# A transformer block on one core: the first four queries computed before the shift, all weight sums on VectorE, modulation weights loaded one group ahead

## The chip, the cores and the metric

The kernel runs on one core of one Trainium2 chip. The metric is the device time of one execution in microseconds (us). All runs named here are fast ones (granted clock 0.995 to 1.0 on the core). A profile is of one execution, so single stretches of it can differ from the median run by a few us.

In the profile PE is TensorE's matmuls, PEld its weight loads, DVE VectorE, ACT ScalarE, POOL GpSimd, SPq the instruction queue of SyncE, which issues nearly all DMAs here. L257 would be line 257 of the program. Line numbers differ between the kernels, because the change adds lines: VectorE's modulation sum is L699 before and L748 after, and the subtraction of weight blocks is L500 before and L541 after.

## The reference

```python
mod = (silu(c) @ w_mod)                     # six rows of 1024: sa, ca, ga, sb, cb, gb
h = layernorm(x) * (1 + ca) + sa            # x: 2048 x 1024, bfloat16
x = x + ga * attention(h)                   # 32 query heads, 4 key heads of 128, last 512 keys
h = layernorm(x) * (1 + cb) + sb
x = x + gb * ((silu(h @ w_gate) * (h @ w_up)) @ w_down)     # 3584 wide
```

The attention projects queries with `wq` (1024 x 4096) and its output with `wo`.

## The kernel before

Tokens are handled in four chunks of 512. In a chunk, 32 heads pass one after another. TensorE works for head `i` (scores, probabilities times values) and for the queries of heads `i+4` and later. From head 8 the queries of two heads come from seven smaller products instead of eight (a Strassen-like scheme), which needs differences of blocks of `wq`, the *weight sums*. They are computed in the first chunk, four per group of four heads, stored to DRAM, and loaded again in later chunks. In the first chunk VectorE also has to move products out of PSUM, normalise the next chunk, and sum up the modulation weights.

```python
def weight_sums(g, st, e, which):            # st, e: the engine; each is 128x1024
    ...
    for k in which:
        x, y, extra = ((b12, b11, []), (b22, t_[:, 0], [bt[0]]), (b22, b12, []), (b21, t_[:, 1], [bt[1]]))[k]
        tt_(st, e, t_[:, k], bt[k], x, y, ALU.subtract, B_wq[sl] + extra)
# in the loop over heads, at the end of head i:
if i % 4 == 3 and i > 3:  load_wq((i + 1) // 4 + 2)         # 1 MB of query weights, two DMAs
g = (i + 6) // 4
if i % 4 == 2 and 2 <= g < HG + 2:
    if g > 2: weight_sums(g, DVE, V, (0,))
    weight_sums(g, POOL, G, (2,))            # GpSimd
g = (i + 5) // 4
if i % 4 == 3 and 2 <= g < HG + 2:
    if g > 2: weight_sums(g, DVE, V, (1,))
    weight_sums(g, POOL, G, (3,))            # GpSimd
if i % 4 == 0 and i >= 4 and (i + 4) // 4 < HG + 2:
    store_sums((i + 4) // 4)                 # 1 MB to DRAM
# at the start of a head in the first chunk:
if h < 12: load_x(TPC + h)                   # 256 KB
if h in (8, 10, 12): load_wo((h - 8) // 2)   # 1 MB of output weights
```

At the start, 2048 columns of `w_mod` (shift and scale, 4 MB) are loaded, and the first query waits for both halves:

```python
for kc in (0, 1, 2, 3, 6, 7):  ln_scale(0, kc, g1, B_g1, sa, B_sa)      # h = n * g1 + sa
...
qproj(0); qproj(1, XBK); turn_keys(); qproj(2); scores(0); qproj(3, XBK)
```

Every instruction is recorded with the semaphores it has to wait for. In the traces below VectorE goes through its list in order: an instruction that could run stands behind one that waits, in one place behind a wait of 4.06 us.

The softmax here doesn't subtract the row's maximum and nothing guards it: scores larger than these inputs give would overflow.

## Time and profile before

| | us |
|---|---|
| median of the four runs beside the changed kernel | 1276.68 (1273.82 to 1279.53) |
| profiled span | 1274.5 |
| first query product | 20.15 |
| first exponential of head 5 to that of head 31 | 104.0 |
| the same 13 pairs of heads at the later chunks' 6.60 us a pair | 85.8 |

The page of the kernel before gives busy time by engine, and then busy tenths in 40 slices of the span:

```profile
PE 1240.5 (97%) x8129; PEld 710.8 (56%) x8269; DVE 622.8 (49%) x1265; ACT 370.4 (29%) x500; POOL 53.9 (4%) x57
...
PE   6988999999999999999999999999999999999999
...
DVE  4888704987048871377504643145422553133421
...
POOL 1322300000000000000000000000000000000000
PEclk9999999999999999999999999999999999999999
```

TensorE is below 9 tenths only within the first four slices (127 us). VectorE is at 4 to 8 tenths there, and GpSimd shows in the first five alone. VectorE's 49% over the whole span says nothing about that stretch.

The timeline of ScalarE of the kernel before (start, duration, what), with the exponentials of heads 5 and 31, and of two heads a pair apart in the second chunk:

```profile
46.33 1.94 ACT L608 ACTIVATE arena<-ps 128x1024 bf16<-128x1024 f32 x2
...
150.29 1.94 ACT L608 ACTIVATE arena<-ps 128x1024 bf16<-128x1024 f32 x2
...
232.45 1.94 ACT L608 ACTIVATE arena<-ps 128x1024 bf16<-128x1024 f32 x2
...
239.06 1.94 ACT L608 ACTIVATE arena<-ps 128x1024 bf16<-128x1024 f32 x2
```

The exponential follows TensorE's scores, so it serves as a clock of the heads: 8.0 us for a pair in the first chunk, 6.6 later.

What TensorE waited for between 20 and 200 us (who, for whom, us in total, times, longest):

```profile
PE ps L259 <- DVE arena L557: 9.2, 6, 2.8
PE ps L259 <- DVE arena L624: 1.6, 3, 0.9
...
```

L557 is a copy of a product out of PSUM. That copy takes 0.42 us, so longer waits mean that VectorE came to it late. Three timelines of one stretch show why: GpSimd's, then VectorE's, then TensorE's, with the wait of 1.58 us in its bracket:

```profile
61.10 2.12 POOL L500 TENSOR_TENSOR arena<-arena 128x1024 f16<-128x1024 bf16 x1 [1.19 <-DVE arena L500]
```

```profile
61.27 2.50 DVE L699 SCALAR_TENSOR_TENSOR arena<-arena 128x512 f32<-128x512 bf16 x1
...
64.15 0.41 DVE L557 COPY arena<-ps 128x256 f32<-128x256 f32 x1
```

```profile
64.62 10.49 PE L259 MATMUL ps<-arena 128*128 128x256 f16 x103 [1.58 <-DVE arena L557]
```

While GpSimd forms its weight sum, VectorE's modulation step, with both inputs in SBUF, takes 2.50 us instead of 0.74. It ends 0.55 us after the sum, so it seems to have stood until GpSimd was done. Beside another sum (at 71.4 us) a subtraction with both inputs in SBUF takes 1.86 us instead of 0.68 and also ends 0.55 us after it, while a multiplication with an operand from PSUM keeps its 0.69. Four of the six waits follow such a stretched instruction; the longest, 2.8 us, has another cause. A second sort of wait, in VectorE's timeline, where the bracket is the idle time before an instruction and what ended it:

```profile
96.42 0.49 DVE L695 TENSOR_SCALAR arena<-arena 128x512 f32<-128x512 bf16 x1 [3.52 <-DMA arena<-in_w_mod_dram]
96.86 0.42 DVE L557 COPY arena<-ps 128x256 f32<-128x256 f32 x1
```

VectorE stands 3.52 us for a load of modulation weights that nobody needs soon. Behind it in the queue stands the copy that TensorE does need: this is the wait of 2.8 us, and from 96.85 us the granted clock is half for 3.41 us.

### The profile page before, as it was taken

The page shows a single profiled execution, that of the slowest core. Times are in us where ns is not written, and L with a number is a line of the kernel's source. Part 1 is how long each engine was busy: PE and PEld are TensorE (multiplying, and loading weights), DVE is VectorE, ACT ScalarE, POOL GpSimd, SP SyncE. Part 2 cuts the span into 40 slices and gives each one's busy share as a digit, 9 for nine tenths or more (in the row PEclk, how much of TensorE's full clock was granted, in tenths as well). Part 3 has the DMA queues.
Part 4 walks back from the last instruction along what each step waited for, and adds up shares of the span by engine and source line. Part 5 has one row for each costly group of instructions (what it writes and reads, how often), then busy time and mean ns, then how long its engine had stood idle before and what let it go on. Part 6 is the DMA issues. An engine that isn't in the chain of part 4 may idle for free.

```text
span 1274.5 us, 20165 instructions
## 1 busy us (share of the span) xinstructions
PE 1240.5 (97%) x8129; PEld 710.8 (56%) x8269; DVE 622.8 (49%) x1265; ACT 370.4 (29%) x500; POOL 53.9 (4%) x57
## 2 busy tenths in 40 slices
PE   6988999999999999999999999999999999999999
PEld 3666645777457774578744444444444444444444
DVE  4888704987048871377504643145422553133421
ACT  2655502676026770177700111011100111011100
POOL 1322300000000000000000000000000000000000
PEclk9999999999999999999999999999999999999999
DMA  7997545997549995488448974036520645024200
GB/s 265 252 313 210 180 136 178 292 255 206 167 159 262 250 216 145 147 238 214 89 147 285 299 215 155 25 83 161 178 92 25 157 148 179 28 83 133 67 9 25
DMA packets 234846, 212.50 MB, mean 167 GB/s; under 512 B 106752, under 2 KB 205952, under 8 KB 230912
## 3 DMA queue, kind: packets, MB, share of 16 engines
q1 hardware_dynamic: 234736, 211.19, 58.3%
q8 instruction: 65, 1.06, 0.4%
q14 instruction: 29, 0.24, 0.1%
q10 hardware_dynamic: 16, 0.00, 0.0%
HBM read 174.07 MB, written 12.58 MB: 146 GB/s over the span
## 4 chain that ended last, share of the span: by engine, by line
PE 94%; DMA 2%; DVE 2%; issue 1%; SPq 0%; ACT 0%; DVEq 0%
PE ps L259 94%; DMA arena<-in_w_mod_dram 2%; DMA arena<-arena 0%; DVE arena L625 0%; SPq L276 0%; DVE arena L342 0%; DVE arena L500 0%; DVE arena L561 0%; DVE arena L557 0%; ACT arena L718 0%; SPq L269 0%; DVE arena L624 0%; DVE arena L594 0%; DVE arena L699 0%; DVE arena L363 0%
## 5 line engine op out<-in xcount | busy, mean ns | idle before, releaser
L259 PE MATMUL ps<-arena 128*128 128x512 bf16 (+4 forms) x8080 | 1236.7, 312 | 27.8 <-DVE arena L557 9.2
L259 PEld LDWEIGHTS ps<-arena 128*128 128x128 bf16 (+1 forms) x8220 | 707.0, 98 | 557.1 <-issue 13.5
L608 ACT ACTIVATE arena<-ps 128x1024 bf16<-128x1024 f32 x256 | 248.1, 1021 | 50.6 <-PE ps L259 47.7
L905 ACT ACTIVATE arena<-ps 128x512 bf16<-128x512 f32 x112 | 66.9, 597 | 518.0 <-PE ps L259 518.0
L635 DVE TENSOR_TENSOR arena<-ps,arena 128x512 bf16<-128x512 f32 (+1 forms) x65 | 44.4, 683 | 338.9 <-PE ps L259 338.9
L906 DVE SCALAR_TENSOR_TENSOR arena<-arena,ps 128x512 bf16<-128x512 bf16 x112 | 77.1, 688 | 142.1 <-ACT arena L905 142.1
L555 ACT ACTIVATE arena<-ps 128x256 f32<-128x256 f32 x120 | 46.0, 383 | 268.1 <-PE ps L259 268.1
L908 DVE SCALAR_TENSOR_TENSOR arena<-arena,ps 128x512 bf16<-128x512 bf16 x112 | 77.0, 687 | 53.7 <-PE ps L259 53.6
L625 DVE TENSOR_TENSOR arena<-ps,arena 128x512 bf16<-128x512 f32 x128 | 88.5, 691 | 4.7 <-DVE arena L624 0.2
L561 DVE TENSOR_TENSOR arena<-ps,arena 128x256 bf16<-128x256 f32 x180 | 75.4, 419 | 6.9 <-PE ps L259 2.2
L349 POOL TENSOR_TENSOR arena<-arena 128x1 f32<-128x1 f32 x32 | 18.2, 570 | 881.1 <-DVE arena L347 881.1
L699 DVE SCALAR_TENSOR_TENSOR arena<-arena 128x512 f32<-128x512 bf16 x56 | 47.2, 843 | 0.0
L624 DVE RECIPROCAL arena<-ps 128x4 f32<-128x4 f32 x128 | 23.1, 180 | 42.8 <-PE ps L259 42.0
L342 DVE BATCH_NORM_STATS2 arena<-arena 128x6 f32<-128x512 bf16 x64 | 43.9, 685 | 0.1
L500 POOL TENSOR_TENSOR arena<-arena 128x1024 f16<-128x1024 bf16 x16 | 34.4, 2149 | 86.4 <-DVE arena L500 45.3
L557 DVE COPY arena<-ps 128x256 f32<-128x256 f32 x60 | 25.2, 419 | 15.5 <-PE ps L259 15.4
L594 DVE CAST arena<-ps 128x256 bf16<-128x256 f32 x60 | 25.2, 420 | 13.3 <-PE ps L259 12.3
L637 DVE TENSOR_TENSOR arena<-arena 128x512 bf16<-128x512 bf16 (+1 forms) x65 | 27.4, 421 | 2.2
L500 DVE TENSOR_TENSOR arena<-arena 128x1024 f16<-128x1024 bf16 (+1 forms) x32 | 25.6, 809 | 0.2
L363 DVE TENSOR_SCALAR arena<-arena 128x512 bf16<-128x512 bf16 x62 | 22.4, 406 | 0.0
L353 DVE TENSOR_SCALAR arena<-arena 128x1024 bf16<-128x1024 bf16 x32 | 17.3, 540 | 2.9 <-DMA arena<-arena 2.4
L495 DVE CAST arena<-ps 128x512 bf16<-128x512 f32 x8 | 5.5, 687 | 7.6 <-PE ps L259 7.6
(31 smaller groups left out, 50.9 us busy)
## 6 DMA issues: line engine op xcount, KB each, us to landing
arena<-in_A_wq_dram SPq DMA_DIRECT2D x64, 512.0 KB, 4.8
arena<-in_A_wo_dram SPq DMA_DIRECT2D x32, 1024.0 KB, 5.3
arena<-in_B_w_gate_dram SPq DMA_DIRECT2D x28, 1024.0 KB, 5.3
arena<-in_B_w_up_dram SPq DMA_DIRECT2D x28, 1024.0 KB, 7.5
arena<-wq_sums SPq DMA_DIRECT2D x22, 1024.0 KB, 7.1
arena<-in_w_mod_dram SPq DMA_DIRECT2D x8, 1024.0 KB, 8.0
wq_sums<-arena SPq DMA_DIRECT2D x8, 1024.0 KB, 6.7
arena<-in_B_w_down_dram SPq DMA_DIRECT2D x4, 1792.0 KB, 11.0
```

What stands on the lines that cost most here:

```text
L259: T.op(PE, lambda: TE.matmul(out_ap, lhsT, rhs, start=start, stop=stop, skip_group_check=loose), reads=reads, writes=bb)
L342: T.op(DVE, lambda: V.bn_stats(st_sb[i][:, 6 * hf:6 * hf + 6], x_sb[:, t, 512 * hf:512 * hf + 512]), reads=[BX[t]], writes=[B_st[i]])
L500: T.op(st, lambda: e.tensor_tensor(dst, x, y, op), reads=reads, writes=[dst_b])
L555: T.op(ACT, lambda: A.activation(sn[k], bank(QBK, 256), AF.Copy), writes=PB[QBK] + [B_sn[k]])
L561: T.op(DVE, lambda: V.tensor_tensor(dst, bank(XBK, 256, off), sn[k], ALU.add), reads=[B_sn[k]], writes=PB[XBK] + [B_q[i % NQ]])
L608: T.op(ACT, lambda: A.activation(ex[i % NEX][:, kt:kt + 2, :], bank(SCB[kt], 1024).rearrange("p (a b) -> p a b", a=2), AF.Exp, scale=att_s ...
L625: T.op(DVE, lambda: V.tensor_tensor(o_sb[i % NOS].rearrange("p (a b) -> p a b", a=TPC), num, rl_bc, ALU.mult), reads=[B_rl], writes=both + ...
L635: T.op(DVE, lambda: V.tensor_tensor(tmp[s][:, 0:n], ps_ap, gate[:, lo:lo + n], ALU.mult), reads=[gate_b], writes=bb + [B_tmp[s]])
L699: T.op(DVE, lambda: V.scalar_tensor_tensor(acc, ms[:, kc, :], sc[:, kc:kc + 1], acc, op0=ALU.mult, op1=ALU.add), reads=[B_ms, B_sc, B_acc] ...
L905: T.op(ACT, lambda: A.activation(th[e], bank(gb_), AF.Tanh, scale=0.5), writes=PB[gb_] + [B_th[e]])
L906: T.op(DVE, lambda: V.scalar_tensor_tensor(out=t1[e], in0=th[e], scalar=1.0, in1=bank(gb_), op0=ALU.add, op1=ALU.mult), reads=[B_th[e]], w ...
L908: T.op(DVE, lambda: V.scalar_tensor_tensor(out=gu[:, ft, :], in0=t1[e], scalar=0.5, in1=bank(ub_), op0=ALU.mult, op1=ALU.mult), reads=[B_t ...
```

## The change

It starts the first four queries on the normalised and scaled but unshifted input, and adds the shift later as one column per head (`wq` transposed times `sa`), so only half of the first modulation load has to be waited for. It moves all weight sums to VectorE, one per head: the first two of each group a head earlier than before, the other two a head later. It loads modulation weights one group ahead and spreads their summing. It moves 14 PSUM copies to ScalarE. The core of the diff:

```diff
-            for kc in range(DT):
-                T.op(Q_wm[kc], lambda: SP.dma_start(wm[:, kc, :], w_mod[kc * P:(kc + 1) * P, 0:2 * D]), writes=[B_wm[kc]])
+            load_wm(0)                       # the scale half; then wq, keys
+            load_wm(1)                       # the shift half
...
-            qproj(0)
-            qproj(1, XBK)
-            turn_keys()
-            qproj(2)
-            scores(0)
-            qproj(3, XBK)
+            q_plain(0, Q0[0], 1)             # on the scaled input, no shift
+            q_plain(1, Q0[1], 1)
+            ... column products of the shift half, q_plain(2), turn_keys() ...
+            for i in range(4):
+                for kc in range(DT):
+                    mm(bank(SFT, 1, DT + i), wq_sb[0][:, kc, hd(i) * P:(hd(i) + 1) * P], sa[:, kc:kc + 1], ...)
+            T.op(DVE, lambda: V.tensor_copy(shift, bank(SFT, 4, DT)), writes=PB[SFT] + [B_shift])
+            for i in range(4):
+                if i == 3:
+                    q_plain(3, Q0[3], 1)
+                T.op(ACT, lambda: A.activation(q_sb[i], bank(Q0[i]), AF.Identity, bias=shift[:, i:i + 1]), ...)
...
-                snap(DVE, 1)
+                snap(ACT if p0 < Hq + LEAD else DVE, 1)
...
-                if h not in (Hq - 5, Hq - 4) and i > 2:
+                if ch == 0:
+                    for g_ in ([ln1[1]] if 1 in ln1 else []) + [mod_ga] * (i > 2) * (1 if i < 8 else i % 2 if i < 20 else 1 + i % 2):
+                        step(g_)
+                elif h not in (Hq - 5, Hq - 4):
                     run()
...
-                if i % 4 == 2 and 2 <= g < HG + 2:
-                    if g > 2:
-                        weight_sums(g, DVE, V, (0,))
-                    weight_sums(g, POOL, G, (2,))
-                (the same with sums 1 and 3 at i % 4 == 3)
-                if i % 4 == 0 and i >= 4 and (i + 4) // 4 < HG + 2:
-                    store_sums((i + 4) // 4)
+                for k in range(4):
+                    g = (i + 7 - k) // 4
+                    if i % 4 == (k + 1) % 4 and (3 if k < 2 else 2) <= g < HG + 2:
+                        weight_sums(g, DVE, V, (k,))
+                if i % 4 == 2 and i >= 6 and (i + 2) // 4 < HG + 2:
+                    store_sums((i + 2) // 4)
```

Cut: layer norm sums of two tiles on ScalarE, buffers and queues for the modulation loads, separate temporaries in `add_to_x`, the two exponentials of a head issued apart. The query-weight loads keep their places.

More of the change, by code (lines that the diff above doesn't have):

```diff
@@ L173, in bufs @@
         return [_Buf("%s%d" % (name, i)) for i in range(n)]
-    AT_WO, AT_OT, AT_X, AT_H, AT_WQ, AT_TQ, AT_S, AT_MS = 0, 24, 56, 88, 104, 120, 136, 144
+    AT_WO, AT_OT, AT_X, AT_H, AT_WQ, AT_TQ, AT_S, AT_MS, AT_FT = 0, 24, 56, 88, 104, 120, 136, 144, 152
     AT_KT, AT_V, AT_EX, AT_Q, AT_OS, AT_GA, AT_GB, AT_N, AT_ACC, AT_TMP, AT_SN, AT_C = (
@@ L194, in bass_adaLN_cond__sliding_block_cached__swiglu_ffn__prompt_kernel @@
     tmp = [M.take((AT_TMP + i) * KB, [512], BF16, [B_tmp[i]]) for i in range(2)]
+    B_rt = bufs("rt", 2)
+    rt = [M.take((205 + i) * KB, [512], BF16, [B_rt[i]]) for i in range(2)]
     cat = [AT_C * KB]
@@ L201, in small @@
         cat[0] += (n * (4 if dtype == F32 else 2) + 63) // 64 * 64
-        assert cat[0] <= 207 * KB
+        assert cat[0] <= 205 * KB
         return ap, b
@@ L219, in bass_adaLN_cond__sliding_block_cached__swiglu_ffn__prompt_kernel @@
     rl, B_rl = small("rl", TPC, F32)
+    xsum, B_xsum = [None] * TPC, [None] * TPC
+    for i in (2, 3):
+        xsum[i], B_xsum[i] = small("xsum%d" % i, 3, F32)
+    shift, B_shift = small("shift", 4, F32)
     st_sb, mv_sb, rs_sb, B_st, B_mv, B_rs = [], [], [], [], [], []
@@ L243, in bass_adaLN_cond__sliding_block_cached__swiglu_ffn__prompt_kernel @@
     Q_x = [dq("q_x%d" % i) for i in range(4)]
-    Q_wm = [dq("q_wm%d" % i) for i in range(DT)]
+    Q_wm = [dq("q_wm%d" % i) for i in range(2 * DT)]
     Q_tr = [dq("q_tr%d" % i) for i in range(4)]
@@ L272, in _, with load_wm @@
                 load_x(t)
-            B_wm = bufs("wm", DT)
-            wm = M.take(AT_OT * KB, [DT, 2 * D], BF16, B_wm)
-            for kc in range(DT):
-                T.op(Q_wm[kc], lambda: SP.dma_start(wm[:, kc, :], w_mod[kc * P:(kc + 1) * P, 0:2 * D]), writes=[B_wm[kc]])
+            B_wm = bufs("wm", 2 * DT)
+            wm = M.take(AT_OT * KB, [2 * DT, D], BF16, B_wm)
+            def load_wm(which):
+                for kc in range(DT):
+                    T.op(Q_wm[which * DT + kc], lambda: SP.dma_start(
+                        wm[:, which * DT + kc, :], w_mod[kc * P:(kc + 1) * P, (1 - which) * D:(2 - which) * D]),
+                        writes=[B_wm[which * DT + kc]])
+            load_wm(0)
             NWQ = 2
@@ L298, in _ @@
                  writes=[B_kn])
+            load_wm(1)
+            load_wq(1)
             VW = 160
@@ L311, in _ @@
                     A_v_cache[0, gk, Sk - W:Sk, :].rearrange("(p k) d -> p k d", k=KT)), writes=[B_vg[gk]])
-            load_wq(1)
             def hd(i):
@@ L390, in ln_task, with mod_open @@
                     yield
-            def mod_open(kc):
-                for j in list(range(DT, 2 * DT)) + list(range(DT)):
-                    mm(bank(QBK, 1, j), wm[:, kc, j * P:(j + 1) * P], sc[:, kc:kc + 1],
-                       kc == 0 and j == DT, kc == DT - 1, [B_wm[kc], B_sc], PB[QBK], loose=True)
+            def mod_open(which, kc, b):
+                for j in range(DT):
+                    mm(bank(b, 1, j), wm[:, which * DT + kc, j * P:(j + 1) * P], sc[:, kc:kc + 1],
+                       kc == 0 and j == 0, kc == DT - 1, [B_wm[which * DT + kc], B_sc], PB[b], loose=True)
             def open_turn(tt):
@@ L401, in open_turn @@
                     transpose(bank_bf(b)[:, kc * P:(kc + 1) * P], n0[tt][:, kc * P:(kc + 1) * P], P, [B_n0[tt]], PB[b])
-                T.op(ACT, lambda: A.activation(h_sb[0][:, :, tt * P:(tt + 1) * P],
-                                               bank_bf(b)[:, 0:DT * P].rearrange("p (a b) -> p a b", a=DT), AF.Copy),
-                     writes=PB[b] + [B_hn[0][tt]], after=B_h[0])
+                dst = h_sb[1][:, :, tt * P:(tt + 1) * P]
+                src = bank_bf(b)[:, 0:DT * P].rearrange("p (a b) -> p a b", a=DT)
+                if tt in (1, 2):
+                    T.op(ACT, lambda: A.activation(dst, src, AF.Copy), writes=PB[b] + [B_hn[1][tt]], after=B_h[1])
+                else:
+                    T.op(DVE, lambda: V.tensor_copy(dst, src), writes=PB[b] + [B_hn[1][tt]], after=B_h[1])
             def keep_warm(n):
@@ L411, in _, with sums_1 @@
             n0 = [M.take((AT_WO + 2 * tt) * KB, [D], BF16, [B_n0[tt]]) for tt in range(TPC)]
-            for tt in range(TPC + 1):
-                if tt < TPC:
-                    ln_stats(tt, tt, 0)
-                    ln_stats(tt, tt, 1)
-                    ln_rstd(tt)
-                if tt:
-                    ln_norm(tt - 1, tt - 1, n0[tt - 1], B_n0[tt - 1])
-            mod_open(0)
+            def sums_1(tt):
+                T.op(ACT, lambda: A.activation(n0[tt], x_sb[:, tt, :], AF.Copy, accum_out=xsum[tt][:, 0:1]),
+                     reads=[BX[tt]], writes=[B_n0[tt], B_xsum[tt]])
+                T.op(DVE, lambda: V.tensor_scalar(xsum[tt][:, 1:2], xsum[tt][:, 0:1], -1.0 / D, None, op0=ALU.mult),
+                     reads=[B_xsum[tt]], writes=[B_xsum[tt]])
+                T.op(ACT, lambda: A.activation(n0[tt], x_sb[:, tt, :], AF.Square, bias=xsum[tt][:, 1:2], accum_out=xsum[tt][:, 2:3]),
+                     reads=[BX[tt], B_xsum[tt]], writes=[B_n0[tt], B_xsum[tt]])
@@ new lines, in sums_2 @@
+            def sums_2(tt):
+                T.op(DVE, lambda: V.tensor_scalar(mv_sb[tt][:, 0:1], xsum[tt][:, 0:1], 1.0 / D, None, op0=ALU.mult),
+                     reads=[B_xsum[tt]], writes=[B_mv[tt]])
+                T.op(DVE, lambda: V.tensor_scalar(rs_sb[tt][:, 0:1], xsum[tt][:, 2:3], 1.0 / D, eps, op0=ALU.mult, op1=ALU.add),
+                     reads=[B_xsum[tt]], writes=[B_rs[tt]])
+                T.op(POOL, lambda: G.tensor_tensor(rs_sb[tt][:, 1:2], rs_sb[tt][:, 0:1], nhalf, ALU.pow),
+                     reads=[B_rs[tt], B_nhalf], writes=[B_rs[tt]])
@@ new lines, in _ @@
+            for tt in range(2):
+                ln_stats(tt, tt, 0)
+                ln_stats(tt, tt, 1)
+                ln_rstd(tt)
+                if tt == 0:
+                    sums_1(2)
+            sums_2(2)
+            ln_norm(0, 0, n0[0], B_n0[0])
+            sums_1(3)
+            ln_norm(1, 1, n0[1], B_n0[1])
+            ln_norm(2, 2, n0[2], B_n0[2])
+            sums_2(3)
+            mod_open(0, 0, QBK)
+            keep_warm(1)
+            mod_open(0, 1, QBK)
+            keep_warm(1)
@@ L420, in _ @@
+            mod_open(0, 2, QBK)
+            keep_warm(1)
             open_turn(0)
-            mod_open(1)
+            mod_open(0, 3, QBK)
             open_turn(1)
-            mod_open(2)
+            mod_open(0, 4, QBK)
+            open_turn(2)
+            mod_open(0, 5, QBK)
             keep_warm(1)
-            mod_open(3)
-            open_turn(2)
-            mod_open(4)
-            keep_warm(2)
-            mod_open(5)
+            mod_open(0, 6, QBK)
+            mod_open(0, 7, QBK)
@@ L430, in _ @@
+            ln_norm(3, 3, n0[3], B_n0[3])
+            T.op(DVE, lambda: V.tensor_scalar(g1, bank(QBK, DT), 1.0, None, op0=ALU.add), writes=PB[QBK] + [B_g1])
+            T.op(DVE, lambda: V.tensor_copy(g1f, g1), reads=[B_g1], writes=[B_g1f])
             open_turn(3)
             keep_warm(1)
-            mod_open(6)
-            keep_warm(2)
-            mod_open(7)
-            T.op(DVE, lambda: V.tensor_scalar(g1, bank(QBK, DT, DT), 1.0, None, op0=ALU.add), writes=PB[QBK] + [B_g1])
-            T.op(DVE, lambda: V.tensor_copy(sa, bank(QBK, DT, 0)), writes=PB[QBK] + [B_sa])
@@ L437, in _ @@
-            T.op(DVE, lambda: V.tensor_copy(g1f, g1), reads=[B_g1], writes=[B_g1f])
-            keep_warm(2)
             for kc in (0, 1, 2, 3, 6, 7):
-                ln_scale(0, kc, g1, B_g1, sa, B_sa)
+                T.op(DVE, lambda: V.tensor_scalar(h_sb[1][:, kc, :], h_sb[1][:, kc, :], g1[:, kc:kc + 1], None, op0=ALU.mult),
+                     reads=B_hn[1] + [B_g1], writes=[B_h[1][kc]])
             for kc in (4, 5):
-                T.op(ACT, lambda: A.activation(h_sb[0][:, kc, :], h_sb[0][:, kc, :], AF.Identity,
-                                               bias=sa[:, kc:kc + 1], scale=g1f[:, kc:kc + 1]),
-                     reads=B_hn[0] + [B_g1f, B_sa], writes=[B_h[0][kc]])
+                T.op(ACT, lambda: A.activation(h_sb[1][:, kc, :], h_sb[1][:, kc, :], AF.Copy, scale=g1f[:, kc:kc + 1]),
+                     reads=B_hn[1] + [B_g1f], writes=[B_h[1][kc]])
@@ L481, in turn_keys @@
                 for i in range(GK):
-                    b = OBK + i // 8
+                    b = SCB[1 + i // 8]
                     transpose(bank_bf(b)[:, (i % 8) * P:(i % 8 + 1) * P], k_nat[:, i // KT, (i % KT) * P:(i % KT + 1) * P], P,
@@ L486, in turn_keys, with q_plain, qproj @@
                     T.op(DVE, lambda: V.tensor_copy(kT[:, 8 * j:8 * j + 8, :],
-                                                    bank_bf(OBK + j)[:, 0:8 * P].rearrange("p (a b) -> p a b", a=8)),
-                         writes=PB[OBK + j] + [B_kT[j]])
-            def qproj(i, b=QBK):
+                                                    bank_bf(SCB[1 + j])[:, 0:8 * P].rearrange("p (a b) -> p a b", a=8)),
+                         writes=PB[SCB[1 + j]] + [B_kT[j]])
+            def q_plain(i, b, slot):
                 sl, hh = (i // 4) % NWQ, hd(i) % 4
                 for kc in range(DT):
-                    mm(bank(b), wq_sb[sl][:, kc, hh * P:(hh + 1) * P], h_sb[0][:, kc, :], kc == 0, kc == DT - 1,
-                       [B_wq[sl][kc // 4], B_h[0][kc]], PB[b])
+                    mm(bank(b), wq_sb[sl][:, kc, hh * P:(hh + 1) * P], h_sb[slot][:, kc, :], kc == 0, kc == DT - 1,
+                       [B_wq[sl][kc // 4], B_h[slot][kc]], PB[b])
+            def qproj(i, b):
+                q_plain(i, b, 0)
                 T.op(DVE, lambda: V.tensor_copy(q_sb[i % NQ], bank(b)), writes=PB[b] + [B_q[i % NQ]])
@@ L564, in _ @@
             late = []
+            LEAD, PLAIN = 4, 8
             def q_first(p0):
@@ L606, in scores, with exps @@
                     mm(bank(SCB[kt]), kT[:, gk * KT + kt, :], q_sb[i % NQ], True, True, [B_kT[gk // 2], B_q[i % NQ]], PB[SCB[kt]])
-                for kt in range(0, KT, 2):
+                exps(i, 0)
+            def exps(i, kt):
+                if i < NA:
                     T.op(ACT, lambda: A.activation(ex[i % NEX][:, kt:kt + 2, :],
@@ L634, in add_to_x @@
             def add_to_x(ps_ap, bb, gate, gate_b, t, lo, n, s):
-                T.op(DVE, lambda: V.tensor_tensor(tmp[s][:, 0:n], ps_ap, gate[:, lo:lo + n], ALU.mult),
-                     reads=[gate_b], writes=bb + [B_tmp[s]])
-                T.op(DVE, lambda: V.tensor_tensor(x_sb[:, t, lo:lo + n], x_sb[:, t, lo:lo + n], tmp[s][:, 0:n], ALU.add),
-                     reads=[B_tmp[s], BX[t]], writes=[BX[t]])
+                T.op(DVE, lambda: V.tensor_tensor(rt[s][:, 0:n], ps_ap, gate[:, lo:lo + n], ALU.mult),
+                     reads=[gate_b], writes=bb + [B_rt[s]])
+                T.op(DVE, lambda: V.tensor_tensor(x_sb[:, t, lo:lo + n], x_sb[:, t, lo:lo + n], rt[s][:, 0:n], ALU.add),
+                     reads=[B_rt[s], BX[t]], writes=[BX[t]])
             def o_bank(ch, k):
@@ L677, in oproj @@
                 load_wo(ch * HG + HG + 2)
-            Q_ms = dq("q_ms")
+            Q_ms = [dq("q_ms%d" % i) for i in range(2)]
+            ms_n = [0]
             def mod_task(groups):
@@ L684, in load @@
                     B_ms = _Buf("ms")
-                    ms = M.take(AT_MS * KB, [DT, 512], BF16, [B_ms])
+                    ms = M.take((AT_FT, AT_MS)[ms_n[0] % 2] * KB, [DT, 512], BF16, [B_ms])
+                    q_ = Q_ms[ms_n[0] % 2]
+                    ms_n[0] += 1
                     col0 = groups[n][0]
-                    T.op(Q_ms, lambda: SP.dma_start(ms, w_mod[:, col0:col0 + 512].rearrange("(k p) n -> p k n", p=P)), writes=[B_ms])
+                    T.op(q_, lambda: SP.dma_start(ms, w_mod[:, col0:col0 + 512].rearrange("(k p) n -> p k n", p=P)), writes=[B_ms])
                     return ms, B_ms
                 nxt = load(0)
-                for _ in range(3):
-                    yield
+                yield
                 for n, (_, what, hf) in enumerate(groups):
                     ms, B_ms = nxt
+                    if n + 1 < len(groups):
+                        nxt = load(n + 1)
                     T.op(DVE, lambda: V.tensor_scalar(acc, ms[:, 0, :], sc[:, 0:1], None, op0=ALU.mult),
@@ L700, in mod_task @@
                              reads=[B_ms, B_sc, B_acc], writes=[B_acc])
-                    if n + 1 < len(groups):
-                        nxt = load(n + 1)
                     yield
@@ L737, in run, with step @@
                             tasks.remove(g_)
+            def step(g_):
+                if g_ in tasks and next(g_, tasks) is tasks:
+                    tasks.remove(g_)
             def finish(g_):
@@ L746, in _ @@
                 mods[name] = [(base * D + 512 * hf, name, hf) for hf in range(2)]
-            qproj(0)
-            qproj(1, XBK)
-            turn_keys()
-            qproj(2)
+            SFT = SCB[0]
+            Q0 = [OBK, OBK + 1, QBK, XBK]
+            q_plain(0, Q0[0], 1)
+            q_plain(1, Q0[1], 1)
+            for kc in range(3):
+                mod_open(1, kc, SFT)
+            q_plain(2, Q0[2], 1)
+            for kc in range(3, DT):
+                mod_open(1, kc, SFT)
+            T.op(DVE, lambda: V.tensor_copy(sa, bank(SFT, DT)), writes=PB[SFT] + [B_sa])
+            turn_keys()
+            for i in range(4):
+                for kc in range(DT):
+                    mm(bank(SFT, 1, DT + i), wq_sb[0][:, kc, hd(i) * P:(hd(i) + 1) * P], sa[:, kc:kc + 1], i == 0 and kc == 0,
+                       kc == DT - 1, [B_wq[0][kc // 4], B_sa], PB[SFT], loose=True)
+            T.op(DVE, lambda: V.tensor_copy(shift, bank(SFT, 4, DT)), writes=PB[SFT] + [B_shift])
+            for i in range(4):
+                if i == 3:
+                    q_plain(3, Q0[3], 1)
+                T.op(ACT, lambda: A.activation(q_sb[i], bank(Q0[i]), AF.Identity, bias=shift[:, i:i + 1]),
+                     reads=[B_shift], writes=PB[Q0[i]] + [B_q[i]])
+            for kc in range(DT):
+                T.op(DVE, lambda: V.tensor_scalar(h_sb[0][:, kc, :], h_sb[1][:, kc, :], sa[:, kc:kc + 1], None, op0=ALU.add),
+                     reads=[B_h[1][kc], B_sa], writes=[B_h[0][kc]])
             scores(0)
-            qproj(3, XBK)
+            exps(0, 2)
             load_wq(2)
@@ L756, in _ @@
             mod_rest = mod_task([m for k_ in ("cb", "sb", "gb") for m in mods[k_]])
+            next(mod_ga)
             tasks.append(mod_ga)
@@ L759, in _ @@
             ln2 = {}
-            LEAD, PLAIN = 4, 8
             o_list = o_start(NCH - 1)
@@ L798, in _ @@
                         q_fourth(p0)
+                exps(i + 1, 2)
                 if h == Hq - 5 and ch + 1 < NCH:
@@ L821, in _ @@
                 g = (i + 6) // 4
-                if i % 4 == 2 and 2 <= g < HG + 2:
-                    if g > 2:
-                        weight_sums(g, DVE, V, (0,))
-                    weight_sums(g, POOL, G, (2,))
-                g = (i + 5) // 4
-                if i % 4 == 3 and 2 <= g < HG + 2:
-                    if g > 2:
-                        weight_sums(g, DVE, V, (1,))
-                    weight_sums(g, POOL, G, (3,))
-                if i % 4 == 0 and i >= 4 and (i + 4) // 4 < HG + 2:
-                    store_sums((i + 4) // 4)
+                for k in range(4):
[4 more added lines that the diff above has]
+                    store_sums((i + 2) // 4)
                 if h == Hq - 1:
@@ L837, in _ @@
                         mod_columns()
+                        next(mod_rest)
                         tasks.append(mod_rest)
```

## The prediction

> **What bounds the kernel.** TensorE: busy 1240.5 of 1274.5 us (page, part 1); the chain that ended last is 94% TensorE. By stretches it is 99% busy from 150 us on. The slack lies before 155 us: the start, and the 32 heads of the first chunk. From the first exponential of head 5 (46.33) to that of head 31 (150.29) is 104.0 us, 8.0 per pair of heads; a pair takes 6.60 in chunk 1 (timeline of ScalarE). 13 pairs lose 18.2 us.
>
> **Where those go** (timeline; waits of TensorE). A GpSimd weight sum takes 2.12 us; a VectorE instruction with SBUF inputs beside it takes 2.50 instead of 0.74 (modulation sum), 2.23 instead of 0.42 (cast), 1.86 instead of 0.68. [...] VectorE works in order, so its copy of a product out of PSUM (L557) comes late: TensorE waits 9.2 us for it in six waits. In one, VectorE stands 3.52 us for a modulation weight load at 92.9 us, after which the granted clock is half for 3.4 us (another 1.7 lost).
>
> **The change, loop.** Takes 16 sums (34 us) off GpSimd, puts them on VectorE at 0.68 (10.9 us); moves 14 copies of 0.42 (5.9 us) to ScalarE, at 0.38; loads modulation weights one group ahead; thins modulation steps to every second head from head 8. VectorE per pair in heads 8 to 18: 3.5 (evictions) + 1.4 (sums) + 1.4 (layer norm) + 0.74 = 7.0 us of durations; successive instructions overlap by about 0.08, so about 6.2 of 6.6 us. ScalarE: 3.9 + 1.14 = 5.0 of 6.6. Of the 18.2 us, 16.5 are removable (1.7 remains in chunk 1 too), and 2 to 4 should stay as short waits: gain 13.5 us.
>
> **The change, start.** The first query product, at 20.15 us, waits for 1 MB of x, 4 MB of modulation weights, then query weights. At the traced 390 GB/s, 2 MB less brings it 5.2 us forward, to about 15; layer norm, partly on ScalarE, just keeps up. But 64 column products of the shift half (2.3 us) now stand after that point, and 32 new ones through the query weights (1.2 us): net 1.7, more or less by when the clock is released (25.2 us now). Eight extra VectorE adds (0.40 each) hide under the fourth query. Start gain 2 us (0 to 4).
>
> **Prediction.** 1276 - 13.5 - 2 = about 1260.5 us, range 1254 to 1268. Chances: faster by over 2% 0.05, within 2% 0.94, slower 0.01.
>
> **What would show it.** GpSimd busy about 20 us instead of 53.9; modulation sums at 0.74 mean in the first chunk; no TensorE wait over 1 us after 30 us; heads 5 to 31 in 88 to 91 us; no clock drop near 95 us; first query product at 14 to 16 us, first exponential at 26.5 to 29.5 (29.3 before).
>
> **What would make it wrong.** VectorE saturating in heads 4 to 18, at 0.3 us a head (gain halved). Weight sums standing on query weights, since they come one head sooner after the load: VectorE would wait for a DMA in order, as at 92.9 us. The start's second stage exposing latency (shift columns, copy, bias). Going beyond 2% is unlikely: all TensorE idle time is 34 us, and most of 10 passes before the first data.

## The result, and the profile after

Measured: 1268.78 us median (1267.81 to 1268.97, four runs) against 1276.68. The ratio is 0.9937 (95% interval 0.9913 to 0.9960). A ratio here is the mean time of one kernel's fast runs over that of the other's of the same rounds, so it is not quite the ratio of the medians. The gain is 7.9 us, about half of the 15.5 foretold, and the time lies 0.8 us above the stated range.

The page after, the same lines:

```profile
PE 1246.4 (98%) x8298; PEld 711.2 (56%) x8298; DVE 613.5 (48%) x1272; ACT 379.2 (30%) x524; POOL 20.0 (2%) x41
...
DVE  4968507886068770476504553245422643234321
...
POOL 1000000000000000000000000000000000000000
PEclk9989999999999999999999999999999999999999
```

GpSimd has lost its sums, and the granted clock has a dip in the third slice. The heads of the first chunk (timeline of ScalarE, heads 5, 14, 16 and 31):

```profile
43.13 1.02 ACT L653 ACTIVATE arena<-ps 128x1024 bf16<-128x1024 f32 x1
...
74.75 1.94 ACT L653 ACTIVATE arena<-ps 128x1024 bf16<-128x1024 f32 x2 [0.48 <-PE ps L265]
...
88.06 1.94 ACT L653 ACTIVATE arena<-ps 128x1024 bf16<-128x1024 f32 x2 [1.32 <-PE ps L265]
...
140.97 1.02 ACT L653 ACTIVATE arena<-ps 128x1024 bf16<-128x1024 f32 x1
```

Heads 5 to 31 take 97.8 us instead of 104.0, and 13.3 of them go into the one pair from head 14 to head 16. TensorE's waits from 26 to 150 us:

```profile
PE ps L265 <- DVE arena L602: 4.0, 1, 4.0
PE ps L265 <- DVE arena L636: 0.9, 3, 0.4
...
```

The six waits of before have gone, and one of 4.0 us has come; the rest of the list is under 1 us each. VectorE's timeline there:

```profile
76.86 0.69 DVE L670 TENSOR_TENSOR arena<-ps,arena 128x512 bf16<-128x512 f32 x1
81.61 0.69 DVE L541 TENSOR_TENSOR arena<-arena 128x1024 f16<-128x1024 bf16 x1 [4.06 <-DMA arena<-in_A_wq_dram]
82.22 0.42 DVE L602 TENSOR_TENSOR arena<-ps,arena 128x256 bf16<-128x256 f32 x1
```

The first weight sum of group 5 stands for its query weights. L602, which TensorE needs, stands behind it in the queue. The queue of SyncE shows what was issued when:

```profile
66.89 0.56 SPq L275 DMA_DIRECT2D arena<-in_A_x_dram  x1
67.50 0.42 SPq L503 DMA_DIRECT2D arena<-in_A_wo_dram  x1
...
69.89 0.57 SPq L552 DMA_DIRECT2D wq_sums<-arena  x1
70.51 0.44 SPq L275 DMA_DIRECT2D arena<-in_A_x_dram  x1
...
72.43 1.16 SPq L299 DMA_DIRECT2D arena<-in_A_wq_dram  x2
73.64 1.44 SPq L503 DMA_DIRECT2D arena<-in_A_wo_dram  x1
```

The view of the query-weight tensor between 66 and 80 us gives the time from issue to landing of those two DMAs:

```profile
DMA to landing us min/median/max: 7.6/8.1/8.5
```

Issued at 72.4 and 73.1, wanted at 77.6, landed at 81.6. Ahead of it in the queue are 1 MB of output weights, the 1 MB store of sums, two tiles of x (0.5 MB) and two transposes (left out of the view above).

The wait costs more than itself. The records of the granted clock put it at half from 81.7 to 88.5 us. TensorE resumes at 82.70, so it works 5.8 us at half speed (its 128x512 products start 0.43 us apart there, and 0.22 after) and loses 2.9. Together that is 4.0 + 2.9 = 6.9 us; the pair took 13.3 - 6.6 = 6.7 more than in later chunks, and a last bit of the half clock falls after it. The drop lasts 6.83 us here; in the kernel before it lasted 3.41. What TensorE did ahead of each drop is in the last section.

With that pair as it should be, the changed kernel would have lain near 1262 us by this sum (1268.8 - 6.9), close to the forecast. The experiments had to show whether that is so, or whether VectorE, with all the sums, was simply full.

### The profile page after: what moved, and what is told of

It is laid out like the page before. It is cut to its first block, busy times and chain, and to the rows that moved or that the text cites. A ratio compares the mean times of both kernels' runs of the same rounds, so it can differ in the third digit from the quotient of the medians.

```text
span 1266.0 us, 20347 instructions
## 1 busy us (share of the span) xinstructions
PE 1246.4 (98%) x8298; PEld 711.2 (56%) x8298; DVE 613.5 (48%) x1272; ACT 379.2 (30%) x524; POOL 20.0 (2%) x41
## 2 busy tenths in 40 slices
DMA packets 235997, 212.49 MB, mean 168 GB/s; under 512 B 106880, under 2 KB 206080, under 8 KB 232064
## 3 DMA queue, kind: packets, MB, share of 16 engines
q1 hardware_dynamic: 235888, 211.19, 59.0%
## 4 chain that ended last, share of the span: by engine, by line
PE 94%; DMA 2%; SPq 1%; DVE 1%; issue 1%; ACT 0%; DVEq 0%
PE ps L265 94%; DMA arena<-wq_sums 1%; DMA arena<-in_w_mod_dram 1%; DMA arena<-in_A_wq_dram 1%; SPq L284 1%; SPq L676 0%; DVE arena L670 0%; DVE arena L602 0%; DVE arena L748 0%; ACT arena L765 0%; DMA arena<-arena 0%; DVE arena L636 0%; SPq L275 0%; DVE arena L669 0%; DVE arena L541 0%
## 5 line engine op out<-in xcount | busy, mean ns | idle before, releaser
L265 PE MATMUL ps<-arena 128*128 128x512 bf16 (+4 forms) x8249 | 1243.1, 313 | 13.3 <-DMA arena<-in_w_mod_dram 4.3
L596 ACT ACTIVATE arena<-ps 128x256 f32<-128x256 f32 x134 | 51.3, 383 | 258.6 <-PE ps L265 254.0
L670 DVE TENSOR_TENSOR arena<-ps,arena 128x512 bf16<-128x512 f32 x128 | 88.5, 692 | 4.7 <-DMA arena<-arena 0.2
L602 DVE TENSOR_TENSOR arena<-ps,arena 128x256 bf16<-128x256 f32 x180 | 75.7, 421 | 11.8 <-PE ps L265 7.0
L748 DVE SCALAR_TENSOR_TENSOR arena<-arena 128x512 f32<-128x512 bf16 x56 | 41.6, 743 | 0.1
L354 DVE BATCH_NORM_STATS2 arena<-arena 128x6 f32<-128x512 bf16 x60 | 41.2, 686 | 0.1
L541 DVE TENSOR_TENSOR arena<-arena 128x1024 f16<-128x1024 bf16 (+1 forms) x48 | 32.4, 683 | 4.2 <-DMA arena<-in_A_wq_dram 4.1
L636 DVE CAST arena<-ps 128x256 bf16<-128x256 f32 x60 | 25.2, 420 | 11.4 <-PE ps L265 10.2
L598 DVE COPY arena<-ps 128x256 f32<-128x256 f32 x46 | 19.4, 422 | 14.6 <-PE ps L265 14.6
L269 PE MATMUL ps<-arena 128*128 128x128 bf16 (+1 forms) x49 | 4.9, 262 | 3.7 <-DVE arena L345 3.7
L358 DVE BATCH_NORM_AGGREGATE arena<-arena 128x2 f32<-128x12 f32 x30 | 6.3, 209 | 1.0
```

Of the source, the lines that this page charges most:

```text
L265: T.op(PE, lambda: TE.matmul(out_ap, lhsT, rhs, start=start, stop=stop, skip_group_check=loose), reads=reads, writes=bb)
L354: T.op(DVE, lambda: V.bn_stats(st_sb[i][:, 6 * hf:6 * hf + 6], x_sb[:, t, 512 * hf:512 * hf + 512]), reads=[BX[t]], writes=[B_st[i]])
L541: T.op(st, lambda: e.tensor_tensor(dst, x, y, op), reads=reads, writes=[dst_b])
L596: T.op(ACT, lambda: A.activation(sn[k], bank(QBK, 256), AF.Copy), writes=PB[QBK] + [B_sn[k]])
L602: T.op(DVE, lambda: V.tensor_tensor(dst, bank(XBK, 256, off), sn[k], ALU.add), reads=[B_sn[k]], writes=PB[XBK] + [B_q[i % NQ]])
L670: T.op(DVE, lambda: V.tensor_tensor(o_sb[i % NOS].rearrange("p (a b) -> p a b", a=TPC), num, rl_bc, ALU.mult), reads=[B_rl], writes=both + ...
```

## The experiments

Theory: the loss is the wait for the query weights and the half clock behind it. Rival: VectorE has no room for what it took over in heads 4 to 18. All runs gave correct results, and each compares with the kernel before in its own rounds.

| run | median us | ratio to before (95%) | heads 5 to 31, us |
|---|---|---|---|
| changed kernel | 1268.78 | 0.9937 (0.9913 to 0.9960) | 97.8 |
| e1_wo_late | 1261.47 | 0.9882 (0.9857 to 0.9907) | 90.8 |
| e2_sums_gpsimd | 1269.47 | 0.9949 (0.9924 to 0.9974) | 100.7 |
| e3_sums_later | 1267.71 | 0.9928 (0.9905 to 0.9951) | 97.0 |
| e4_before_dve | 1275.49 | 0.9997 (0.9971 to 1.0023) | 104.1 |
| e5_one_wo_late | 1267.28 | 0.9915 (0.9884 to 0.9947) | 97.6 |
| e6_mod_each_head | 1260.87 | 0.9864 (0.9839 to 0.9889) | 90.7 |
| e7_copies_vector | 1260.73 | 0.9865 (0.9840 to 0.9890) | 91.8 |
| e8_best | 1261.95 | 0.9871 (0.9844 to 0.9898) | 93.3 |
| e9_two_wo_late | 1264.01 | 0.9904 (0.9881 to 0.9927) | 93.9 |
| e10_store_behind | 1271.26 | 0.9961 (0.9944 to 0.9978) | 98.8 |
| e11_sums_mid | 1269.05 | 0.9949 (0.9932 to 0.9966) | 100.1 |
| e12_sums_mid_wo | 1264.27 | 0.9910 (0.9895 to 0.9925) | 94.2 |

e1 to e4, e5 to e8, and e9 to e12 each shared a chip and the runs of before (medians 1275.16, 1277.03, 1276.62). The last column is from the one profiled execution, which for e11 is its slowest run (1272.54).

### The output-weight loads moved away

```diff
-                    if h in (8, 10, 12):
-                        load_wo((h - 8) // 2)
+                    if h in (18, 22, 26):
+                        load_wo((h - 18) // 4)
```

> The changed kernel with the three output-weight loads moved from heads 8, 10, 12 to heads 18, 22, 26. Theory (a weight sum of group 5 stands 4.1 us for a query-weight load that took 8.5 us to land in a crowded stretch of DMA, TensorE waits 4.0 us behind it, and the clock is then half for 6.8 us, 3.4 us more): the wait and the clock drop vanish, 7 us less than the changed kernel, about 1261.5 us, wait of VectorE for query weights under 0.5 us. Rival (VectorE is simply full in heads 4 to 18 with the sums it took over): moving these loads does not lighten VectorE, so the time stays within 2 us of 1268.8.

Measured: 1261.47 us, as the theory said. The query weights of group 5 land after:

```profile
DMA to landing us min/median/max: 4.6/5.1/5.5
```

VectorE's waits from 26 to 150 us, the whole list:

```profile
DVE arena L669 <- PE ps L265: 7.3, 15, 1.2
DVE arena L602 <- PE ps L265: 5.8, 9, 1.0
DVE arena L536 <- PE ps L265: 1.8, 1, 1.8
DVE arena L636 <- PE ps L265: 0.7, 2, 0.3
```

No DMA is left among what VectorE waits for, TensorE's longest wait there is 0.4 us, the clock never drops in the loop, and the pair from head 14 takes about 6.6 us. VectorE's work is the same as in the changed kernel, so the rival falls as the cause of these 7 us (e3 and e4 show where it does hold). This version beats both kernels.

### The third load alone, then the other two

```diff
-                    if h in (8, 10, 12):
-                        load_wo((h - 8) // 2)
+                    if h in (8, 10, 18):
+                        load_wo(min((h - 8) // 2, 2))
```

> The changed kernel with only the third output-weight load (1 MB, issued 1.2 us after the query-weight load that came late) moved from head 12 to head 18; the loads of heads 8 and 10 stay. Theory [...]: landing falls from 8.5 to about 6 us, wait of VectorE from 4.1 to about 1 us, no half clock; 1262 to 1264 us. Rival (the traffic ahead of it, the sums' store at 69.9 and the loads of heads 8 and 10, fills the engines): landing stays above 7 us, 1266 us or more.

Measured: 1267.28 us, nothing gained beyond 1.5 us of round-to-round difference. The landing time is the same with the load behind it taken away:

```profile
  DVE arena L541: 4.0, 1
...
DMA to landing us min/median/max: 7.7/8.1/8.5
```

My theory, that the load issued behind the late one delays it, failed, and the rival, the traffic ahead, held. So the next run left that load at head 12 and moved the other two:

```diff
+                    if h in (12, 18, 22):
+                        load_wo({18: 0, 22: 1, 12: 2}[h])
```

> The changed kernel with the first two output-weight loads moved from heads 8 and 10 to heads 18 and 22, the third left at head 12. Moving the third alone did nothing, so the theory is now that the traffic ahead of the query-weight load delays it (the load of head 10, issued 5 us before, and the store of the sums, 2.5 us before): landing about 6 us, VectorE's wait under 1 us, no half clock, 1261 to 1263 us. Rival (it is the sum of all three loads): landing stays above 7 us, above 1265 us.

```profile
  DVE arena L541: 0.8, 1
...
DMA to landing us min/median/max: 5.1/5.6/6.1
```

Landing fell to 6.1 us and the wait to 0.8; no clock drop. The time, 1264.01, is 1 us above the expectation, since the next group's weights (group 6) made VectorE wait another 2.0 us in the profiled run. In this stretch what was issued ahead delayed the load and what was issued behind did not. The DMA packets in the traces show it directly. The query weights are the only packets of 1024 bytes there. In the changed kernel the first of them moves at 77.7 us, 5.3 us after the issue, when the store's packets of 8192 bytes (74.1 to 76.4) and the tile and most of the transpose behind it have gone. In e5 it is again 5.3 us, in e9 1.9 and in e1 1.8. In the profile page's list of queues one queue, q1, carries 235888 of the changed kernel's 235997 packets.

### The store of the sums behind the query-weight load

```diff
-                if i % 4 == 2 and i >= 6 and (i + 2) // 4 < HG + 2:
-                    store_sums((i + 2) // 4)
+                if i % 4 == 3 and i >= 7 and (i + 1) // 4 < HG + 2:
+                    store_sums((i + 1) // 4)
```

> The changed kernel with the 1 MB store of the sums one head later, behind the query-weight load instead of 2.5 us ahead of it; the output-weight loads stay at heads 8, 10, 12. Theory (traffic ahead; the change itself put this store ahead of the load, before it came after): landing about 6 us, VectorE waits under 1.5 us for it, 1261 to 1264 us. If only the output-weight loads matter: landing stays above 7.5 us, about 1268 us. Possible new cost: the next sums wait for the store to have read their tile.

Landing fell to 6.5 us as the theory has it, with the output weights still at heads 8, 10 and 12. But VectorE now waits for the store itself, which has to read the tile before the next sums may overwrite it:

```profile
DVE arena L541 <- DMA wq_sums<-arena: 5.8, 3, 5.4
```

1271.26 us: the wait was moved, not removed, and the half clock of 6.8 us came with it. Each of the two orders tried in that stretch left VectorE waiting for a DMA that it needed. Taking traffic out (e1, e9) removed most or all of the wait; so does asking for the weights later (e3, next), at another price.

### The sums back on GpSimd, or on VectorE in pairs

Two runs of the changed kernel that differ in the engine alone. Both have sums 0 and 2 at heads 2 mod 4 and sums 1 and 3 at heads 3 mod 4, as before. The first has 2 and 3 on GpSimd, and its theory was that the stretching beside GpSimd is what most of the loop's 18 us went to (an estimate from the trace before):

```diff
+                if i % 4 == 2 and 2 <= g < HG + 2:
+                    if g > 2:
+                        weight_sums(g, DVE, V, (0,))
+                    weight_sums(g, POOL, G, (2,))        # e3: DVE, V
+                (the same with sums 1 and 3 at i % 4 == 3; the store at i % 4 == 0)
```

> The changed kernel with the weight sums as before: sums 2 and 3 of each group on GpSimd, the others one head later. Theory [...]: two-input VectorE instructions beside a GpSimd sum again take 1.9 to 2.5 us, heads 5 to 31 take about 98 us again (collisions back, 8 us; wait for query weights and half clock gone, 7.4 us), total 1267 to 1272 us. Rival (VectorE full): VectorE gets 10.9 us of work less, so clearly faster than the changed kernel, below 1263 us.

> The changed kernel, all sums on VectorE, but two at a time and later as before (0 and 2 at heads 2 mod 4, 1 and 3 at heads 3 mod 4): one head more from the issue of the query-weight load to its first use. Theory: the 4.1 us wait and the clock drop vanish; pairs of sums make bursts of 1.2 us on VectorE that may cost 1 to 2 us in short waits; about 1262 to 1263 us. Rival (VectorE full): the same work on VectorE in coarser pieces, so no better than 1268 us.

On GpSimd: 1269.47 us. VectorE's SBUF instructions are stretched again; its groups by form from 28 to 150 us (count, busy us, mean ns):

```profile
L541 DVE TENSOR_TENSOR arena<-arena 128x1024 f16<-128x1024 bf16 x21 | 18.8, 904 | 0.3 <-DMA arena<-in_A_wq_dram 0.2
L602 DVE TENSOR_TENSOR arena<-ps,arena 128x256 bf16<-128x256 f32 x41 | 17.2, 419 | 8.1 <-PE ps L265 7.9
L748 DVE SCALAR_TENSOR_TENSOR arena<-arena 128x512 f32<-128x512 bf16 x14 | 12.8, 914 | 0.1
```

The mean of L748 is 744 ns in the changed kernel, and that of L541 682; L602, which reads PSUM, is unchanged (420). Of instructions with one input in SBUF some are held too: a scaling of 128x1024 took 2.05 us instead of 0.54 (at 45.1 us), while a layer-norm statistic kept its 0.68 (at 60.5 us). So the stretching beside GpSimd is real. Its price, with all else equal, is heads 5 to 31 in 100.7 instead of 97.0 us, 3.7 us in these profiles. The medians differ by 1.8 us (every run of e2 lies above every run of e3). The two profiles differ by 2.7: 0.8 in the start and 3.7 in the loop, of which later chunks gave 1.7 back. The 8 us that I had expected from collisions was too much.

On VectorE in pairs: 1267.71 us, where I expected 1262 to 1263. The wait for query weights is gone and the clock stays whole, so the theory's first half holds, but heads 5 to 31 take 6.1 us more than in e1. The time is within 0.3 us of what the rival had forecast (no better than 1268). e3 and e1 differ in the place of the output-weight loads too, but no wait of TensorE or VectorE for query weights is left in either. TensorE's waits for other engines from 28 to 155 us add up to 8.0 us in e3 and 1.9 in e1, and all of the difference is behind VectorE's evictions. The table of stretches shows where. The three lines are heads 8 to 10, 10 to 12 and 12 to 14. Each has the stretch, length, busy us (and instructions) of PE, PEld, DVE, ACT, POOL, then granted clock, DMA share, GB/s. First one sum a head (e1), then sums in pairs (e3):

```profile
53.76:60.56 6.80, 6.71 (x68) 5.19 (x68) 6.07 (x14) 4.92 (x7) 0.00 (x0) 1.00 1.16 235
60.56:67.79 7.23, 6.73 (x68) 5.17 (x68) 6.36 (x16) 4.92 (x8) 0.99 (x1) 1.00 1.36 316
67.79:74.65 6.86, 6.71 (x68) 5.19 (x68) 6.42 (x16) 4.92 (x7) 0.55 (x1) 1.00 0.93 273
```

```profile
54.14:62.19 8.05, 6.90 (x68) 5.11 (x68) 7.25 (x17) 5.03 (x7) 0.00 (x0) 1.00 1.20 248
62.19:68.93 6.74, 6.69 (x68) 5.26 (x68) 5.28 (x14) 4.92 (x7) 0.99 (x1) 1.00 1.11 334
68.93:77.12 8.19, 6.90 (x68) 5.11 (x68) 7.67 (x19) 5.03 (x7) 0.55 (x1) 1.00 1.12 297
```

VectorE has the same work over four heads, but 7.25 and 7.67 us of it fall into one pair and 5.28 into the next. The full pair takes 8.1 us, over TensorE's 6.6; the light one takes 6.7, because TensorE cannot go faster than its own work. What a busy stretch loses, the idle one beside it does not give back. "Full" has to be asked pair by pair, and one sum a head is what makes VectorE fit.

### One part alone on the kernel before

```diff
-                    weight_sums(g, POOL, G, (2,))
+                    weight_sums(g, DVE, V, (2,))
 (and the same for sum 3; nothing else)
```

> The kernel before with one part of the change alone: all weight sums on VectorE. Theory: the collisions go (six stretched VectorE instructions, 1.3 to 1.8 us each in TensorE waits, 8 to 9 us), the modulation wait of 3.5 us with the clock drop stays or grows, since modulation weights are still loaded late: about 1268 us (1265 to 1271). Rival (VectorE full): the older kernel has more VectorE work still, so the gain is under 3 us, 1273 us or more.

Measured: 1275.49 us, no gain, though GpSimd is as idle as in the changed kernel (19.6 us busy). The theory (1265 to 1271) missed; the rival's forecast (gain under 3 us, 1273 or more) came true. VectorE's DMA waits:

```profile
DVE arena L695 <- DMA arena<-in_w_mod_dram: 5.5, 1, 5.5
...
DVE arena L500 <- DMA arena<-in_A_wq_dram: 1.4, 1, 1.4
```

The wait for late modulation weights grew from 3.5 to 5.5 us, now 1.4 us of query weights came in, and the sums stand in pairs. TensorE waits 4.8 us behind the modulation weights, with a half clock of 3.41 us after it, and 7.0 us in eleven short waits for other instructions of VectorE. So the run does not refute the rival: with the sums in pairs VectorE comes late, and a load is late as well. In this kernel moving the sums alone did not pay; the runs above have it with the spreading and the earlier loads. The parts of this change are not worth a sum of separate gains.

### The other two measures for VectorE, taken back

Both on e1. First the modulation steps at every head (`[mod_ga] * (i > 2)`), then the 14 copies back on VectorE (`snap(DVE, 1)`).

> The kernel with the three loads moved (e1) with the modulation steps at every head again, instead of every second from head 8 to 19. Theory (VectorE just fits: 6.2 of 6.6 us per pair): with one step of 0.74 us more per pair it is over, 6.9 of 6.6 us; heads 8 to 20 lose 2 to 4 us, heads after 20 gain back 0 to 1; 1263 to 1265 us. Rival (spare time enough; the thinning was not needed): 1261.5 us, same as e1.

> The kernel with the three loads moved (e1) with the 14 copies of the first chunk back on VectorE (0.42 us each) instead of ScalarE. Theory: VectorE at 6.5 of 6.6 us per pair, and a copy stands in its queue behind sums: 2 to 5 us of TensorE waits, 1263.5 to 1266.5 us, waits on that copy in the list. Rival (no matter where): 1261.5 us.

Measured: 1260.87 and 1260.73 us, both as e1. With steps at every head, heads 12 to 20 take 1.0 us more (27.9 against 26.9) and heads 20 to 31 1.1 us less (38.1 against 39.2). The copies cost 1.0 us in heads 5 to 31, which the medians don't show. My expectations of 2 to 5 us were wrong. VectorE has more room than I gave it: with the sums one to a head and the loads moved, either measure can go. Taking both back at once was not run.

### Another place for the sums, and a try at better

```diff
+                for k in range(4):                       # one head later, and before the second product
+                    g = (i + 6 - k) // 4
+                    if i % 4 == (k + 2) % 4 and (3 if k < 2 else 2) <= g < HG + 2:
+                        weight_sums(g, DVE, V, (k,))
                 pv(i, mod_columns if i % 2 else lambda: None)
```

> The changed kernel with one sum a head as there, but half a head to one head later: each sum stands before the second product of its head instead of after it. All DMA traffic as in the changed kernel. Theory (one sum a head is what keeps VectorE from bursts, and one head more is what the load needs): no wait for query weights over 0.5 us and no half clock, heads 5 to 31 in 90 to 92 us, 1261 to 1263 us. If pairs of sums were not what cost 6 us in the run with sums later, but their lateness, this one is slow too: 1266 us or more.

> Both: sums as in the run before this and the three output-weight loads at heads 18, 22, 26. Meant to be the best version: if one remedy is enough, the second adds nothing, 1260.5 to 1262 us; it should be no slower than e1 (1261.5).

Measured: 1269.05 and 1264.27 us, both misses. In e12 TensorE waits 5.0 us in eight waits for the weight sums themselves, 1.0 at most: seven of the eight are for the fourth sum of a group, which now ends just before the product that reads it. In e11 the waits for query weights return too (6.1 us in two, the longest at a later group). There VectorE's `pv` eviction stands behind a sum that waits: TensorE loses 3.7 us at once, and the clock drops for 3.41 us. A sum has to be ready before its product and must leave nothing urgent behind it, and the place at the end of the head, which the change chose, is the better one. Because these two runs were slow for reasons of their own, they do not decide between pairs and lateness in e3; the waits listed there do.

```diff
-            mod_open(0, 7, QBK)                           # e8, on e1
             ln_norm(3, 3, n0[3], B_n0[3])
+            open_turn(3)
+            mod_open(0, 7, QBK)
...
-                elif h not in (Hq - 5, Hq - 4):
+                elif h not in (Hq - 5, Hq - 4) and not (ch == 2 and h < 4):
```

> Meant to beat e1: the three loads moved, the fourth tile of x turned before the last column products of the first modulation half, and no background steps in the first four heads of the third chunk, so that a 1 MB modulation load no longer stands beside the load of the sums TensorE waited 1.3 us for. Expected: first query product about 0.6 us earlier, that wait gone: 1259.7 us (1258 to 1261.5). If the wait was not from the modulation load, only the first: about 1261.

Measured: 1261.95 us, no better than e1. The first query product came at 15.52 us (15.90 in e1). TensorE's wait for reloaded sums (1.3 us in e1's third chunk) did go, but it is absent in e2 and e5 too, which kept the modulation load there, and 0.4 to 0.9 us in other runs. So that the modulation load caused it is not shown. And in the profiled run 2.3 us of waits for query weights came up at two groups. Why they landed later there, with the same loads in the same order, stays open. The margin between landing and use is small even in e1.

## Why the prediction was wrong

- **What bounds the kernel: right. Where the loop loses: the causes exist, their sizes were wrong.** The waits of before are gone, VectorE's modulation sums take 744 ns in the mean (1149 before), GpSimd is busy 20.0 us, as foretold. The size I read into the collisions was too large: the engine alone is worth 3.7 us in heads 5 to 31 (e2 against e3), and of the six waits in the first trace only four, 5.9 us, were collisions. The larger part came from the spreading: one sum a head instead of pairs gives 6.1 us more (e3 against e1, whose loads differ too).
- **"2 to 4 should stay as short waits: gain 13.5 us": this term failed.** Heads 5 to 31 gained 6.1 us (104.0 to 97.8). Missing are 7.0 us: 4.0 behind one wait for a DMA and 2.9 by the half clock. e1 takes exactly this away: heads 12 to 20 in 26.9 us instead of 33.9, heads 5 to 31 in 90.8, a loop gain of 13.1, and 1261.47 us in all, with the forecast at 1260.5. That 13.1 comes so near to 13.5 is in part luck, as its parts are not those that the sum had.
- **The cause was named, and not counted.** The last paragraph lists "weight sums standing on query weights" as a risk, but the sum gave it nothing, and I did not compare the times. Before, the longest landing of these weights between 40 and 150 us was 6.2 us, with less crowding; the changed kernel leaves 5.1 us from issue to use. I also missed that the change puts the 1 MB store in front of that load (behind it again, in e10, the load landed after 6.5 us). That faster heads crowd the same traffic into less time may add to it; no run shows this alone.
- **What hid it before.** GpSimd stood for the same loads, and TensorE's list of waits has none for GpSimd: nothing urgent was behind it. Its waits in the kernel before from 28 to 150 us; the longest is its first and only idling:

```profile
POOL arena L500 <- DMA arena<-in_A_wq_dram: 28.9, 4, 24.4
```

  The other three make 4.5 us. With the sum, such a wait moved to an engine on which TensorE depends. A busy-time account does not see that.
- **"No TensorE wait over 1 us after 30 us": wrong**, by this one event. The clock drop near 95 us went as foretold, but a longer one came at 81.7.
- **VectorE fits in heads 8 to 18: right**, with more room than I thought (e7 adds 0.42 us a pair at no cost in the medians).
- **The start: right within what one can tell.** First query product at 15.52 (14 to 16 foretold), first exponential at 28.21. By head 5 the changed kernel's profile was 3.2 us ahead (46.33 to 43.13), against 2 foretold. But the same start took 42.8 to 45.7 us to head 5 over the profiles of the experiments, and the old one 44.9 in e4. The means (43.7 of eleven profiles, 45.6 of two) differ by 2. Much of the scatter goes with the clock. Its records show it full from 25.2 us on in the kernel before, whose query matmuls start 0.43 us apart until then and 0.22 after, and from 13.4 in the changed kernel. The release came at 12.8 to 13.7 us in the five fastest of the new starts with a record of it (head 5 at 42.8 to 43.3). It came at 21.7 in the slowest (e11, 45.7), no sooner to head 5 than the old start with release at 22.3 (e4, 44.9). So part of the gain here seems to be an earlier clock, which the prediction named ("more or less by when the clock is released") and did not size. Whether the new start brings it is not settled: it was not undone by itself.
- From head 31 to the end the changed kernel lost 0.8 us again (9.3 ahead at head 31, 8.5 at the end); a wait of 0.9 us for reloaded sums in the third chunk, absent before, is of that size. It comes and goes between runs.

## What to carry to other kernels

Before moving work onto an in-order engine, move its waits in thought as well: for each moved instruction compare the time from the issue of its data to its first use with the landing time in that stretch, and look at what stands behind it in the queue. Ask whether an engine fits stretch by stretch, since a burst loses what the calm beside it does not return; here one piece per step was worth more (6.1 us) than the engine it ran on (3.7). When a load comes late, look at what is issued ahead of it and take traffic out of that stretch (landing after 5.5 us in e1 instead of 8.5); the one reordering tried here (e10) handed the wait to another DMA. And a wait costs more than itself when the clock drops behind it: 4.0 us became 6.9.

## Measured, not explained: the clock and the crowded load

- The granted clock dropped with TensorE not idle for the whole stretch ahead of the drop: after 1.19 us of work in the 3.45 us before it in the kernel before (one wait of 2.8 us), and after 0.40 of 3.40 in the changed one (wait of 4.0). In e9 a wait of 2.0 us caused no drop. In the starts of e2 and e6 the clock fell at 24.8 us without a wait longer than 0.6 us; in e6 TensorE is shown 2.39 us busy of the 3.40 before, mostly with one-column products. In e1, with 3.01 us busy in the same stretch, the clock stayed. What makes it fall was not tested.
- What a crowded stretch does to a load: 1 MB of query weights landed after 8.5 us behind 2.5 MB and two transposes issued in the 5.5 us before it, still after 8.5 with the 1 MB behind it taken away, after 6.1 with the output-weight loads of heads 8 and 10 moved, and after 5.5 with all three moved (up to 6.8 in the other runs with all three moved).
